# A fused threshold attention and MLP mixer: four PSUM banks shared out anew between values, turned x and the MLPs

## The chip, the cores and the metric

The kernel runs on one core of one Trainium2 chip. The metric is the device time in microseconds (us), the median of three runs. A profiled execution is a separate run, with its own time; the profile's span goes from the first to the last instruction of the program.

## The reference

For each of 8 batch rows there are 8 heads with 576 tokens and 64 features per head. Attention with a threshold comes first, then a mixer's token MLP and channel MLP, all in float32:

```python
scores = scale * np.matmul(q, k.transpose(0, 1, 3, 2))
thresh = np.max(scores, axis=-1, keepdims=True) - tau
scores = np.where(scores >= thresh, scores, -1000000000.0)
scores = scores - np.max(scores, axis=-1, keepdims=True)
attn = np.exp(scores)
attn = attn / (np.sum(attn, axis=-1, keepdims=True) + 1e-09)
x = np.matmul(attn, v)                       # heads side by side: (8, 576, 512)
h = np.maximum(x.transpose(0, 2, 1) @ w_tok1, 0.0) @ w_tok2
u = x + h.transpose(0, 2, 1)
out = u + np.maximum(u @ w_ch1, 0.0) @ w_ch2
```

The token MLP goes 576 to 256 to 576, the channel MLP 512 to 1536 to 512.

## The kernel before, in words

**Units.** Work on attention is cut into 144 units (L85), 18 for each of the 8 rows. A unit is 128 tokens of two heads; of nine units of two pairs of heads the fifth (SHARED, L86) holds the last 64 tokens of both pairs. The loop at L513 goes once through all units and writes out the order of each engine's work by hand (manual_schedule, L81): each engine runs its instructions in the order in which this loop emits them.

**One turn of the loop**, for unit u: `scores(u)` (TensorE's matmuls at L286, VectorE's maximum at L291, GpSimd's bias at L292); `norm(u-1)` (L310 to L314); `turn_blocks(u-2)`, which turns the weights of unit u-2 by VectorE in blocks of 32 (L348) and by 16 DMAs on SyncE's queue (L358), or, for row 0, `turn`, which does it by TensorE through PSUM (L337, L339); `fill(0.4)`; steps of the conversion of the MLPs' weights (`weight`, L544 and L556); `weigh(u)` on ScalarE (Prelu L301 and Exp L304, two each); `fill(0.3)`; `values` for what is due (L549 to L553); `fill(0.3)`; loads.

**Values.** `values(b, p, c)` (L370) multiplies turned weights with v for one pair of heads and 256 tokens, ten matmuls per half (L388, L393), into one tile of pool `ps_tr`; ScalarE copies it into xT (L398). For c == "s", the last 64 tokens, a unit makes two entries in `due` (L541), so `values` is called for pair p and for pair p+1 directly one after the other; these appear as `pv_s` in the profile. All other entries become due in different units.

**MLPs.** When a row's last values have been emitted, `push(b)` (L497) puts that row's MLP steps into `todo`: five of `turn_x` (transposes of x through a `ps_tr` tile, L412, copied by ScalarE, L413), two of `tok1` (L422, Relu on ScalarE L423), eight of `tok2` (L429, added to xT by VectorE, L433), and steps of the channel MLP, `ch1` (L451, Relu on ScalarE L452) and `ch2` (L463 and L467, in four parts that share one tile, copied by VectorE, L472). Steps left over from the row before are interleaved one to one with the new token MLP's (L502 to L504). `fill` takes steps from `todo` by their estimated costs, so that they are spread over the next 17 units; after the last row the rest follows in one stretch. Each tok1, tok2, ch1 and ch2 takes one tile of pool `ps_mm`.

**PSUM.** All matmul results go to PSUM, in tiles of up to 512 floats per partition, one bank each. `ps_sc` (L73) has two tiles of two banks for scores; `ps_tr` (L74) two of one bank; `ps_3rd` (L78) one of two banks, a third scores buffer in row 0 alone. At unit UB = 18, where row 1 begins (L515), `ps_3rd` is closed and `ps_mm` opens with two tiles in its place. A tile of a pool can be written again when the engine that empties it is through with its former use; where a pool's tiles are all in use, the next matmul waits, and so does all that stands behind it on TensorE.

Of the kernel before, what the change touches and what calls it, by code (L numbers as in the profile page):

```python
# [21 lines left out]
def kernel(  # L22
# [48 lines left out]
    work = ctx.enter_context(tc.tile_pool(name="work", bufs=2))  # L71
    small = ctx.enter_context(tc.tile_pool(name="small", bufs=6))
    ps_sc = ctx.enter_context(tc.tile_pool(name="ps_sc", bufs=2, space=bass.MemoryType.PSUM))  # L73
    ps_tr = ctx.enter_context(tc.tile_pool(name="ps_tr", bufs=2, space=bass.MemoryType.PSUM))  # L74


    late = ctx.enter_context(ExitStack())
    ps_3rd = late.enter_context(tc.tile_pool(name="ps_3rd", bufs=1, space=bass.MemoryType.PSUM))  # L78
    ps_mm = None

# [6 lines left out]
    UB = 9 * NP // 2  # L87
# [128 lines left out]
    def weight(n):  # L216

        nonlocal steps_done
        for _ in range(n):
            if next(wops, wops) is wops:  # L220
                return
            steps_done += 1
# [37 lines left out]
    def in_blocks(b):  # L260
        return b > 0
# [10 lines left out]
    def scores(u):  # L272
        b, p0, t = units[u]
        sc = [
            (ps_3rd if b == 0 and (2 * u + h) % 3 == 2 else ps_sc).tile([P, 2, MAIN], F32, tag="sc", name=f"sc{h}_{u}") for h in range(2)
        ]
        if t == SHARED:
            parts = [(b * NP + p0 + i, slice(MAIN, S), slice(64 * i, 64 * i + 64)) for i in range(2)]
        else:
            i, c = divmod(t - (t > SHARED), NI)  # L280
            parts = [(b * NP + p0 + i, slice(P * c, P * c + P), slice(0, P))]
        order = [(f, part, h) for f in range(2) for part in parts for h in range(2)]
        for f, (n, cols, rows), h in order if b else sorted(order, key=lambda o: o[2]):
            r = slice(D * h, D * h + D)
            qT, kT = heads[n]
            nc.tensor.matmul(sc[h][rows, f, 0:HS], lhsT=qT[r, cols], rhs=kT[r, HS * f : HS * f + HS], start=True, stop=True)  # L286
        mx = small.tile([P, 2], F32, tag="mx", name=f"mx_{u}")
        bias = small.tile([P, 2], F32, tag="bias", name=f"bias_{u}")
        for h in range(2):
            c = slice(h, h + 1)  # L290
            nc.vector.tensor_reduce(out=mx[:, c], in_=sc[h][:, :, 0:HS], axis=AX.XY, op=ALU.max)  # L291
            nc.gpsimd.tensor_scalar(out=bias[:, c], in0=mx[:, c], scalar1=toff, scalar2=-SCALE, op0=ALU.add, op1=ALU.mult)  # L292
        st[u] = sc, bias
# [13 lines left out]
    def norm(u):  # L307
        e, rs = st[u]
        rr = small.tile([P, 2], F32, tag="rr", name=f"rr_{u}")
        nc.vector.tensor_scalar(out=rr, in0=rs, scalar1=1e-9, scalar2=None, op0=ALU.add)  # L310
        nc.vector.reciprocal(out=rr, in_=rr)  # L311
        for h in range(2):
            eh = e[:, S * h : S * h + S]
            nc.gpsimd.tensor_scalar(out=eh, in0=eh, scalar1=rr[:, h : h + 1], scalar2=1.0, op0=ALU.mult, op1=ALU.mult)  # L314
        st[u] = e

    def group_of(u):

        b, p0, t = units[u]
        if t == SHARED:  # L320
            return (b, p0, "s"), 0, 1
        i, c = divmod(t - (t > SHARED), NI)
        return (b, p0 + i, c // 2), c % 2, 2

    def turn(u, third):

        key, place, n = group_of(u)
        e = st[u]
        if third == 0 and place == 0:
            eTs[key] = work.tile([P, NK * 2 * P], F32, tag="eT", name=f"eT_{u}")  # L330
        if third == 2:
            st.pop(u)
        eT = eTs[key][:, 0 : NK * n * P].rearrange("p (c x) -> p c x", c=NK)
        ps = ps_tr.tile([P, MAIN], F32, tag="tr", name=f"tr{third}_{u}")[:, 0 : 3 * P].rearrange("p (c x) -> p c x", c=3)
        for c in range(3):
            k0 = (3 * third + c) * P
            nc.tensor.transpose(out=ps[:, c, :], in_=e[:, k0 : k0 + P], identity=ident)  # L337
        on = nc.scalar.copy if third == 1 and u % 2 else nc.vector.tensor_copy
        on(out=eT[:, 3 * third : 3 * third + 3, P * place : P * place + P], in_=ps)  # L339

    def turn_blocks(u):

        key, place, n = group_of(u)
        e = st.pop(u)
        if place == 0:
            Ts[key] = work.tile([P, NK * 2 * P], F32, tag="T", name=f"T_{u}")
        T = Ts[key][:, 0 : NK * n * P]
        nc.vector.transpose(  # L348
            out=T.rearrange("p (a c n x) -> p c a n x", a=4, c=NK, n=n)[:, :, :, place, :],
            in_=e.rearrange("p (c a x) -> p c a x", c=NK, a=4),  # L350
        )
        if place == n - 1:
            del Ts[key]
            eTs[key] = work.tile([P, NK * 2 * P], F32, tag="eT", name=f"eT_{u}")
            w = NK * n * 32
            for a in range(4):
                for i in range(4):
                    nc.sync.dma_start(  # L358
                        out=eTs[key][32 * a : 32 * a + 32, w * i : w * i + w], in_=T[32 * i : 32 * i + 32, w * a : w * a + w]
                    )  # L360

    def split_middle(n):

        lv, vl = vals[n], vlast[n % VL]
        for h in range(2):
            r = slice(D * h, D * h + D)
            nc.gpsimd.tensor_copy(out=vl[r, r], in_=lv[r, NI, :])
        vals[n] = lv, vl
# [118 lines left out]
    def fill(share):  # L487
        nonlocal credit
        credit += share * quota
        while todo and credit > 0:  # L490
            cost, step = todo.popleft()
            credit -= cost
            step()
        if not todo:
            credit = 0.0

    def push(b):  # L497
        nonlocal quota
        uT = xTs[b]
        steps, old = token_mlp(b), list(todo)  # L500
        todo.clear()
        for i in range(max(len(steps), len(old))):  # L502
            todo.extend(old[i : i + 1])
            todo.extend(steps[i : i + 1])  # L504
        for i in range(2) if b % 2 == 0 else range(2, (2 * S + GR - 1) // GR):
            todo.extend(channel_mlp(b - b % 2, uT, i))
        quota = (sum(c for c, _ in todo) - (KEEP if b else 0.0)) / (UB - 1)
# [4 lines left out]
    LAG = 2  # L512
    for u in range(len(units) + LAG + 4):  # L513
        on = u < len(units)
        if u == UB:  # L515
            late.close()
            ps_mm = ctx.enter_context(tc.tile_pool(name="ps_mm", bufs=2, space=bass.MemoryType.PSUM))
        if on:
            b_now, p0, t = units[u]
            n = b_now * NP + p0  # L520
        w = u - LAG
        back = 0 <= w < len(units)
        if on:
            scores(u)
        if 0 < u <= len(units):
            norm(u - 1)
        if back:
            key, place, many = group_of(w)
            if in_blocks(key[0]):
                turn_blocks(w)  # L530
            else:
                for i in range(3):
                    turn(w, i)
            if place == many - 1:
                b, p, c = key
                if c == 0 and p % 2 == 0:
                    split_middle(b * NP + p)
                if c == "s":
                    split_middle(b * NP + p + 1)
                when = u + (2 if in_blocks(b) else 1)  # L540
                due += [(when, b, p + i, c) for i in range(2 if c == "s" else 1)]  # L541
        if b_now:
            fill(0.4)
        weight(4 if b_now else 1)  # L544
        if on:
            weigh(u)
        if b_now:
            fill(0.3)
        while due and due[0][0] <= u:  # L549
            _, b, p, c = due.popleft()  # L550
            values(b, p, c)
            if p == NP - 1 and c == 1:
                push(b)  # L553
        if b_now:
            fill(0.3)
        weight(3 if b_now else 1)  # L556
        if on:
            m = n + 2 + t // 4
            if t < 8 and m < len(pairs):
                load_qk(m, (nc.scalar if b_now else nc.sync,) * 2, t % 4)  # L560
                if t % 4 == 3:
                    load_v(m)
            if t == 2:
                prep(n + 1)
            if t == 7 and n + 2 < len(pairs):
                prep(n + 2)
# [31 lines left out]
```

## Time and profile before

| what | value |
|---|---|
| median of three runs | 1418.58 us (1417.44 to 1421.64) |
| profiled execution, its own time | 1424.03 us |
| its span | 1421.9 us |
| granted TensorE clock, mean | 0.984 |
| VectorE busy | 584.1 us |
| ScalarE busy | 589.8 us |
| GpSimd busy | 345.4 us |
| L398, copies of values: 128x256 | 64, mean 373 ns |
| L291, maximum of scores on VectorE | 288, mean 751 ns |
| L451, ch1 matmuls | 1920, 406.2 us busy |
| L467, ch2 matmuls | 864, 389.5 us busy |

How to read it: PE is TensorE's matmuls, PEld its weight loads, DVE VectorE, ACT ScalarE, POOL GpSimd, SP SyncE, which here only issues DMAs. A row names a line of the kernel, an engine, an operation, what is written and read (out<-in) and the shapes; then come the busy time, the mean duration, and the engine's idle time just before such instructions with what ended most of it. Each float32 matmul of the code shows as two matmul instructions in the profile, a transpose as one. "PE t L429 <- DVE xT L433" means that a matmul at L429 had to wait until an instruction at L433 on VectorE ended. The clock is given as a share of full speed.

### The profile page before, as it was taken

The page shows a single profiled execution, that of the slowest core. Times are in us where ns is not written, and L with a number is a line of the kernel's source. Part 1 is how long each engine was busy: PE and PEld are TensorE (multiplying, and loading weights), DVE is VectorE, ACT ScalarE, POOL GpSimd, SP SyncE. Part 2 cuts the span into 40 slices and gives each one's busy share as a digit, 9 for nine tenths or more (in the row PEclk, how much of TensorE's full clock was granted, in tenths as well). Part 3 has the DMA queues.
Part 4 walks back from the last instruction along what each step waited for, and adds up shares of the span by engine and source line. Part 5 has one row for each costly group of instructions (what it writes and reads, how often), then busy time and mean ns, then how long its engine had stood idle before and what let it go on. Part 6 is the DMA issues. An engine that isn't in the chain of part 4 may idle for free.

```text
span 1421.9 us, 19495 instructions
## 1 busy us (share of the span) xinstructions
PE 1346.7 (95%) x6866; PEld 832.4 (59%) x6866; DVE 584.1 (41%) x1009; ACT 589.8 (41%) x1328; POOL 345.4 (24%) x681
## 2 busy tenths in 40 slices
PE   6777689988999999999999999999999999999998
PEld 4443455645656566565656566566657466566675
DVE  5888654344344443434433444334333443201000
ACT  5776353443545444353434444353334344220110
POOL 4565332222222222222212222222121222100000
PEclk9998899989999999999999999999999999999999
DMA  6344544443444434443343534443433433300000
GB/s 130 90 117 131 152 125 103 92 116 84 102 120 111 108 84 106 104 98 80 92 101 77 121 80 111 104 98 69 103 87 83 111 91 78 82 15 15 8 8 23
DMA packets 257376, 128.34 MB, mean 90 GB/s; under 512 B 208064, under 2 KB 221376, under 8 KB 257280
## 3 DMA queue, kind: packets, MB, share of 16 engines
q1 hardware_dynamic: 131632, 111.46, 29.9%
q10 hardware_dynamic: 125648, 15.64, 6.9%
q8 instruction: 55, 0.90, 0.3%
q14 instruction: 41, 0.34, 0.1%
HBM read 43.25 MB, written 9.44 MB: 37 GB/s over the span
## 4 chain that ended last, share of the span: by engine, by line
PE 81%; DVE 8%; SPq 5%; DMA 3%; ACT 3%; issue 1%; POOL 0%; DVEq 0%; ACTq 0%
PE c L467 26%; PE c L451 24%; PE sc L286 10%; PE pv L393 7%; SPq L358 5%; PE t L422 3%; PE t L429 3%; DVE mx L291 3%; PE pv L388 2%; DVE T L348 2%; PE tx L412 2%; PE c L463 1%; DMA eT<-T 1%; DMA scratch<-in_moe_w_ch_dram 1%; ACT e L301 1%
## 5 line engine op out<-in xcount | busy, mean ns | idle before, releaser
L451 PE MATMUL c<-xT,wc 128*128 128x256 f32 (+1 forms) x1920 | 406.2, 363 | 1.9 <-DVE xT L433 0.8
L291 DVE TENSOR_REDUCE mx<-sc 128x1 f32<-128x576 f32 x288 | 204.6, 751 | 489.5 <-PE sc L286 489.4
L467 PE MATMUL c<-wc,g 128*128 128x512 f32 x864 | 389.5, 597 | 0.0
L451 PEld LDWEIGHTS c<-xT,wc 128*128 128x128 f32 x1920 | 331.7, 190 | 75.9 <-issue 29.9
L292 POOL TENSOR_SCALAR bias<-mx,toff 128x1 f32<-128x1 f32 x288 | 76.7, 267 | 807.8 <-DVE mx L291 754.1
L301 ACT ACTIVATE e<-sc,bias 128x576 f32<-128x576 f32 x288 | 199.2, 741 | 169.7 <-POOL bias L292 148.8
L467 PEld LDWEIGHTS c<-wc,g 128*128 128x128 f32 x864 | 157.6, 190 | 177.3 <-issue 175.9
L452 ACT ACTIVATE g<-c 128x256 f32<-128x256 f32 (+1 forms) x240 | 87.3, 364 | 386.0 <-PE c L451 366.5
L304 ACT ACTIVATE e<-e,ntau 128x576 f32<-128x576 f32 x288 | 220.8, 774 | 0.0
L314 POOL TENSOR_SCALAR e<-e,rr 128x576 f32<-128x576 f32 x288 | 213.4, 753 | 17.3 <-DVE rr L311 4.1
L286 PE MATMUL sc<-kT,qT 64*128 64x288 f32 (+1 forms) x1280 | 196.7, 441 | 20.0 <-ACT e L301 10.9
L348 DVE STREAM_TRANSPOSE T<-e 128x1152 f32<-128x1152 f32 x126 | 172.5, 1369 | 16.5 <-DMA eT<-T 10.8
L286 PEld LDWEIGHTS sc<-kT,qT 64*128 64x128 f32 (+1 forms) x1280 | 107.1, 181 | 102.1 <-issue 50.1
L393 PE MATMUL pv<-eT,lv 128*64 128x256 f32 x1024 | 124.0, 385 | 0.0
L472 DVE COPY o<-c 128x512 f32<-128x512 f32 x36 | 24.6, 684 | 192.7 <-PE c L467 192.7
L393 PEld LDWEIGHTS pv<-eT,lv 128*64 128x64 f32 x1024 | 75.7, 140 | 38.0 <-issue 2.6
L429 PE MATMUL t<-w,a 128*128 128x288 f32 x256 | 78.8, 437 | 17.8 <-DVE xT L433 15.8
L422 PE MATMUL t<-x,w 128*128 128x512 f32 (+1 forms) x160 | 76.0, 613 | 0.0
L429 PEld LDWEIGHTS t<-w,a 128*128 128x128 f32 x256 | 46.7, 197 | 42.6 <-DVE xT L433 20.8
L398 ACT COPY xT<-pv 128x256 f32<-128x256 f32 x64 | 23.9, 373 | 107.4 <-PE pv L393 107.3
L433 DVE TENSOR_TENSOR xT<-xT,t 128x288 f32<-128x288 f32 x64 | 27.9, 442 | 96.5 <-PE t L429 96.4
L304 ACT ACTIVATION_READ_ACCUMULATOR e<-e,ntau 128x1 f32 x288 | 57.4, 199 | 0.0
(43 smaller groups left out, 600.4 us busy)
## 6 DMA issues: line engine op xcount, KB each, us to landing
eT<-T SPq DMA_DIRECT2D x896, 72.0 KB, 2.0
scratch<-in_moe_w_ch_dram SPq DMA_DIRECT2D x24, 512.0 KB, 3.8
lv<-in_v_dram SPq DMA_DIRECT2D x32, 288.0 KB, 3.3
out_dram<-o SPq DMA_DIRECT2D x36, 256.0 KB, 2.2
eT<-T SPq DMA_DIRECT2D x224, 36.0 KB, 1.9
lk<-in_k_dram ACTq DMA_DIRECT2D x108, 72.0 KB, 2.7
lq<-in_q_dram ACTq DMA_DIRECT2D x104, 72.0 KB, 2.1
lq<-in_q_dram SPq DMA_DIRECT2D x24, 72.0 KB, 3.3
```

Of the source, the lines that this page charges most:

```text
L286: nc.tensor.matmul(sc[h][rows, f, 0:HS], lhsT=qT[r, cols], rhs=kT[r, HS * f : HS * f + HS], start=True, stop=True)
L291: nc.vector.tensor_reduce(out=mx[:, c], in_=sc[h][:, :, 0:HS], axis=AX.XY, op=ALU.max)
L301: nc.scalar.activation(out=eh, in_=sc[h][:, :, 0:HS], func=AF.Prelu, bias=bias[:, h : h + 1], scale=SCALE, alpha=STEEP)
L304: nc.scalar.activation(out=eh, in_=eh, func=AF.Exp, bias=ntau, accum_out=rs[:, h : h + 1])
L314: nc.gpsimd.tensor_scalar(out=eh, in0=eh, scalar1=rr[:, h : h + 1], scalar2=1.0, op0=ALU.mult, op1=ALU.mult)
L348: nc.vector.transpose(out=T.rearrange("p (a c n x) -> p c a n x", a=4, c=NK, n=n)[:, :, :, place, :], in_=e.rearrange("p (c a x) -> p c a ...
L393: nc.tensor.matmul(to[r], lhsT=lv[:, j, :], rhs=eT[:, j], start=False, stop=(c == NI - 1), skip_group_check=True)
L422: nc.tensor.matmul(ps, lhsT=w1[0:M, t, P * m : P * m + P], rhs=s["x"][0:M, t, :], start=(t == 0), stop=(t == NT - 1))
L429: nc.tensor.matmul(ps, lhsT=s["a"][:, m, P * c : P * c + P], rhs=w2[:, m, HS * f : HS * f + HS], start=(m == 0), stop=(m == NTK - 1))
L451: nc.tensor.matmul(ps, lhsT=wc1[:, j, c, :], rhs=uT[:, c, GR * i : GR * i + n], start=(c == 0), stop=(c == NCC - 1))
L452: nc.scalar.activation(out=s["g"][:, j, 0:n], in_=ps, func=AF.Relu)
L467: nc.tensor.matmul(flat, lhsT=s["g"][:, j, P * t : P * t + P], rhs=wc2[:, j, :], start=False, stop=(j == NJ - 1), skip_group_check=True)
```

## The change

`ps_tr` is opened in the stack of pools that is closed later, under the name ps_tr0, still with two tiles; it serves row 0. The switch of pools moves from the top of unit 18 to the place just before `push(0)`, in unit 20, after row 0's last values have been emitted. From there on `ps_tr` has one tile and `ps_mm` three. Row 0's values and row 0's turned weights use ps_tr0; row 0's turned x, and values and turned x of all later rows, use the single tile. `ps_sc` stays as it is. No instruction is added, removed or reordered.

```diff
-    ps_tr = ctx.enter_context(tc.tile_pool(name="ps_tr", bufs=2, space=bass.MemoryType.PSUM))
+
 
 
     late = ctx.enter_context(ExitStack())
+    ps_tr = late.enter_context(tc.tile_pool(name="ps_tr0", bufs=2, space=bass.MemoryType.PSUM))
     ps_3rd = late.enter_context(tc.tile_pool(name="ps_3rd", bufs=1, space=bass.MemoryType.PSUM))
     ps_mm = None
...
-        if u == UB:
-            late.close()
-            ps_mm = ctx.enter_context(tc.tile_pool(name="ps_mm", bufs=2, space=bass.MemoryType.PSUM))
...
             values(b, p, c)
             if p == NP - 1 and c == 1:
+                if b == 0:
+                    late.close()
+                    ps_tr = ctx.enter_context(tc.tile_pool(name="ps_tr", bufs=1, space=bass.MemoryType.PSUM))
+                    ps_mm = ctx.enter_context(tc.tile_pool(name="ps_mm", bufs=3, space=bass.MemoryType.PSUM))
                 push(b)
```

## The prediction

> **What bounds the kernel now.** I read the page first, then TensorE's list of waits, then the instructions in order of time at the places where tiles of the two pools that change follow each other. Four lines of the page:
>
> ```profile
> PE 1346.7 (95%) x6866; PEld 832.4 (59%) x6866; DVE 584.1 (41%) x1009; ACT 589.8 (41%) x1328; POOL 345.4 (24%) x681
> ...
> PEclk9998899989999999999999999999999999999999
> ...
> PE 81%; DVE 8%; SPq 5%; DMA 3%; ACT 3%; issue 1%; POOL 0%; DVEq 0%; ACTq 0%
> ...
> L429 PE MATMUL t<-w,a 128*128 128x288 f32 x256 | 78.8, 437 | 17.8 <-DVE xT L433 15.8
> ```
>
> TensorE is busy 95% of the span and 81% of the chain that ended last, at full clock in nearly all of the 40 slices. A change of PSUM pools adds no instruction, so it can only move TensorE's waits. The stage list says where waits are left: 250 to 1300 us has TensorE busy 1033.10 of 1050.00 us, while 107 to 178 us (the beginning of row 1) has it busy only 50.26 of 71. In the long stretch each microsecond that TensorE stands still is a microsecond of the result. All its waits after 200 us:
>
> ```profile
> PE pv L388 <- DMA eT<-T: 5.5, 2, 4.9
> PE t L429 <- DVE xT L433: 4.8, 6, 1.6
> PE sc L286 <- ACT e L301: 3.3, 2, 2.0
> PE t L429 <- ACT g L452: 1.8, 5, 0.4
> PE c L451 <- DVE xT L433: 0.8, 1, 0.8
> ```
>
> (columns: who waited for whom, us in all, times, longest). Waits of t L429 and c L451 for L433 or L452 are waits for a ps_mm bank: tok2 reads nothing that L433 writes. That is 7.4 us, all the idle time that a third ps_mm bank can take away after 200 us. Waits for a ps_tr bank do not appear here at all: two banks are always enough. The question is what one does.
>
> [...] a 0.21 us copy of a finished tile starts only after four activations that were queued earlier. [...] before, the second values group indeed runs before the first is copied. [...] after a wait of 2.0 us it granted 0.50 from 194.60 to 198.00, after one of 1.32 us again from 324.30 to 327.70, and yet after one of 1.60 us (338.59) it did not.
>
> **The change part by part.** (1) *Values and turned x on one bank.* A group on ps_tr may now begin only when ScalarE has copied the group before it. From row 1 on these groups come one at a time, in different units, except in the shared unit: there L550 runs values twice in a row (heads p and p+1 of the last 64 tokens). That is two pairs a row, 14 in rows 1 to 7. TensorE at one of them:
>
> ```profile
> 494.63 0.34 PE L388 MATMUL pv_s<-eT,vl 128*64 128x64 f32 x4
> 494.80 0.64 PE L393 MATMUL pv_s<-eT,lv 128*64 128x64 f32 x16
> 495.26 0.29 PE L388 MATMUL pv_s<-eT,vl 128*64 128x64 f32 x4
> 495.38 0.64 PE L393 MATMUL pv_s<-eT,lv 128*64 128x64 f32 x16
> ```
>
> and ScalarE at the same time:
>
> ```profile
> 494.74 0.60 ACT L423 ACTIVATE a<-t 128x512 f32<-128x512 f32 x1 [6.56 <-PE t L422]
> 495.23 1.37 ACT L301 ACTIVATE e<-sc,bias 128x576 f32<-128x576 f32 x2
> 496.48 0.79 ACT L304 ACTIVATE e<-e,ntau 128x576 f32<-128x576 f32 x1
> ...
> 497.24 0.78 ACT L304 ACTIVATE e<-e,ntau 128x576 f32<-128x576 f32 x1
> ...
> 498.00 0.33 ACT L398 COPY xT<-pv_s 128x64 f32<-128x64 f32 x2
> ```
>
> (start us, us, instruction). The second group starts at 495.26. With one bank it waits for the first copy, 498.00 + 0.21 = 498.21: 2.95 us, plus the 0.05 us that lie between the end of a copy and the matmul that it releases (copy over at 126.46, matmul at 126.51). Behind it on TensorE stands everything else, the next scores too, and nothing covers it. I measured all 14 pairs like this. Where ScalarE is free (281.39, 574.44, 653.79, 740.56, 980.80, 1066.85, 1226.10) the wait is 0.43 us: 7 x 0.43 = 3.0. Where the copy is behind the unit's Exp (203.25, 357.34, 896.69: 1.29 each; 423.13: 1.10) it is 5.0. Where tok1's Relu holds back all of weigh (495.26, 821.30, 1147.63) it is 2.95 each, 8.9. With 14 x 0.05 = 0.7 the **pairs cost 17.5 us**.
>
> Turned x: at the end of row 1 (312.52) five tx groups follow pv(row end) at 0.9 us distance or less, since the copy of one lies under the transposes of the next. On one bank each takes its transposes (0.6 to 0.9), the copy (0.59) and two hand-overs: I get 313.04 for the first and 317.6 in place of 315.6 for the end of the fourth, **2.0 us**. In later rows push interleaves them with older steps, and five collisions are left: 470.69 and 795.25 (0.53 each), 614.72 and 938.27 (the copy waits behind weigh, 1.72 each), 1119.66 (0.74): **5.2 us**. In row 0's chain tx 0 now waits for the copy as well (it ran at 121.17, ahead of the 4.7 us wait), and tx 1 to 4 follow 1.3 to 1.5 us apart and not 0.9: 2.7 us. TensorE waits 8.0 us for VectorE soon after, so part may vanish there: between 0 and 2.7, I take **1.5**.
>
> (2) *Three banks for the MLPs.* After 350 us the bank waits sum to 4.8 us; [...] nearly all of them are waits for the group just before, so a free bank removes them: **-6**. The two 1.60 us waits of row 2 (338.59, 346.68) are a third tok2 waiting for the first's add, which VectorE reaches late. A third bank lets one more tok2 of 0.97 us run; then the fourth waits: **-1.9**. Row 1's waits of 8.0 and 3.0 us are the same, but VectorE there is held at 151.14 by a weight load, so again one tok2 moves into the wait. It ran at half clock afterwards (eight matmuls from 152.72 took 4.21 us, 2.1 per tok2), so 2.1 + 1.9 at most; I take **-3**, between 0 and 18 (both waits and the half clock after them gone). The sum is -11, from -6 to -26.
>
> (3) *The clock.* Nine waits of over 1 us appear in stretches at full clock. Each may cost a 3.4 us window at half clock, 1.7 us. Of the waits of 1.3 to 2.0 us that the trace has after 180 us about half were followed by such a window. I count three quarters for the three long ones and 0.3 for six shorter: 4 windows, **+7**, from 0 to 15.
>
> (4) *The switch moved from unit 18 to 20* costs nothing: ps_mm is first used after push(0) either way, and turned x of row 0 needs the last values of that row anyhow. Evictions stay where they are in the queues; no DMA moves.
>
> Sum: 17.5 + 2.0 + 5.2 + 1.5 - 11 + 7 = +22 us on the profiled execution of 1424.03 us (span 1421.9). That execution lies 5.45 us above the median, so 1424.03 + 22 - 5.45 = **1440.6 us**, which I give as 1440. Its own range, with the pairs and the row 1 and later tx waits (24.7) as measured: from +7 (row 0's chain 0, gains 18, clock 0) to +34 (2.7, 6 and 13), 1426 to 1453.
>
> **The rivals.** *The clock becomes the bound* (slower still): every one of the nine waits draws a half-clock window, 9 x 1.7 = 15.3, and gains stay at 6: 17.5 + 7.2 + 2.7 - 6 + 15.3 = +37, 1455. For it speaks the window at 324.30 after only 1.32 us idle; against it the three waits of 1.6 to 1.75 us without one.
>
> *Row 1 gives back more than the pairs take* (faster). Row 1 is the one stage where TensorE is idle by tens of microseconds, because tok2 stands before the next scores in its queue. If one more bank lets these scores go early enough, 8.0 + 3.0 us and the half clock after them (10.24 and 3.41 us at 0.50, so 6.8) go, with 8 of the rest: -26. If row 1 and 2 also swallow their own pairs (4.1 with 203.25, 281.39, 357.34 and 423.13) and tx chains (3.5), 17 us of cost is left before the clock's: -9, 1410. It decides if over two thirds of the 11 us go. Against it: the add is released by a weight load, not by a bank.
>
> *A draw*: gains of about 19 (bank waits of the page, 15.8 + 1.8 + 0.8 + 0.6) against 24.7 without any clock loss, part absorbed: +2, 1420.
>
> That the pools do not do what they say can be excluded for ps_tr: with bufs=1 no second bank exists.
>
> **How the numbers follow.** Forecast 0.62, clock 0.20, draw 0.10, row 1 faster 0.08. The range 1424 to 1455 takes in the forecast, the clock case and the upper part of the draw. A measurement of this kernel can tell about 0.3% (4.3 us) from no change: faster 0.08, same 0.10, slower 0.82.
>
> **What would show it.** Right: in TensorE's waits a new row, pv_s L388 for ACT xT L398, 14 times and 15 to 18 us, longest near 3; tx L412 for ACT x L413; t L429 for DVE xT L433 down to a few us after 200 us; some more half-clock windows. Wrong: no such row, or 107 to 178 us much shorter, or pairs far from 1.2 us in the mean because the order of ScalarE's work has shifted.

## The result and the profile after

The changed kernel takes 1445.08 us (median of 5 runs, 1442.14 to 1447.06); before took 1420.28 us beside it (5 runs, 1417.44 to 1421.64). The ratio is 1.0166, 95% interval 1.014 to 1.0192: 24.8 us slower. The forecast was 1440 us, on a median of 1418.58.

From the pages: in the changed kernel's file every line from the pool definitions on has moved down by one, so tok2 is L430 and not L429, and its add L434.

```profile
PE 1351.5 (94%) x6866; PEld 837.2 (58%) x6866; DVE 583.1 (40%) x1009; ACT 589.3 (41%) x1328; POOL 346.8 (24%) x681
...
L430 PE MATMUL t<-w,a 128*128 128x288 f32 x256 | 75.0, 421 | 7.9 <-DVE xT L434 7.9
```

No engine has other work: the counts are equal, and busy times differ by under 5 us. The span grew from 1421.9 to 1443.0 us. tok2's idle time before its matmuls fell from 17.8 to 7.9 us: the third bank did what it was there for. What was added is in TensorE's waits after 200 us (who waited for whom, us in all, times, longest):

```profile
PE pv_s L389 <- issue: 14.8, 13, 2.9
PE tx L413 <- ACT x L414: 5.1, 5, 1.6
PE pv L389 <- DMA eT<-T: 4.4, 1, 4.4
PE sc L287 <- ACT e L302: 3.3, 2, 2.0
PE tx L413 <- ACT xT L399: 1.4, 3, 0.5
PE pv_s L389 <- POOL wc L169: 1.2, 1, 1.2
PE pv L389 <- issue: 0.7, 1, 0.7
PE c L452 <- DVE xT L434: 0.6, 1, 0.6
PE t L430 <- DVE xT L434: 0.6, 1, 0.6
```

The first row is new and is the largest: 13 waits before the second values group of a pair, and the 14th is the row with L169, 16.0 us in all. The list does not name the releaser here ("issue", and once a GpSimd instruction that has nothing to do with it); the instructions in order of time do. TensorE at the pair that the prediction showed:

```profile
507.10 0.34 PE L389 MATMUL pv_s<-eT,vl 128*64 128x64 f32 x4 [2.87 <-issue]
507.23 0.67 PE L394 MATMUL pv_s<-eT,lv 128*64 128x64 f32 x16
507.83 2.08 PE L452 MATMUL c<-xT,wc 128*128 128x128 f32 x8
```

and ScalarE:

```profile
506.03 0.78 ACT L305 ACTIVATE e<-e,ntau 128x576 f32<-128x576 f32 x1
506.69 0.20 ACT L305 ACTIVATION_READ_ACCUMULATOR e<-e,ntau 128x1 f32 x1
506.79 0.21 ACT L399 COPY xT<-pv_s 128x64 f32<-128x64 f32 x1
507.94 0.21 ACT L399 COPY xT<-pv_s 128x64 f32<-128x64 f32 x1 [0.94 <-PE pv_s L394]
```

The first copy ends at 507.00 behind the second Exp, and the second group starts at 507.10. Before, both copies ran back to back behind the Exp (0.33 us from 498.00), and TensorE had begun on the ch1 matmuls behind them at 495.95. Behind the wait the granted clock is 0.50 from 507.80 to 511.20 us, and eight ch1 matmuls take 2.08 us where they took 1.16.

Where the 21.1 us of span come from can be read by taking the two traces (one execution each) matmul by matmul, since the order on TensorE is the same in both. The table has the differences of start-to-start times, in us; the 14 pairs come to more than their 16.0 us of waits because each place loses another 0.16 us beside the wait:

| place | measured | in the prediction |
|---|---|---|
| 14 pairs: 7 x 0.53, 3 x 1.38, 1.23, 3.04 + 3.05 + 3.04 | +18.2 | 17.5 |
| turned x in row 1's end (0.73, 0.70, 0.63) | +2.1 | 2.0 |
| five later turned x collisions (0.54, 1.72, 0.54, 1.72, 0.79) | +5.3 | 5.2 |
| turned x of row 0 | +3.8 | 1.5, from 0 to 2.7 |
| tok2 in row 1 (-8.20, -0.40 and +5.98; -3.18 and +1.15) | -4.7 | -3 |
| tok2 in row 2 (-1.76 + 0.79, -1.77 + 0.80) | -1.9 | -1.9 |
| MLP bank waits after 350 us, those over 0.3 us | -5.9 | -6 |
| granted clock of 0.50, four stretches from 330 us on (1.6, 1.6, 0.87, 0.90) | +5.0 | 7 |

These sum to +21.9. Another 2.0 us of the span lie before row 1, where the two programs are the same, so they are scatter between two executions, and the rest (-2.8) is in smaller pieces, some of opposite sign, which I did not attribute. The prediction's -6 for the MLP banks stands on 4.8 us of waits; the rest of it was an estimate of such a loss beside each wait.

### The profile page after: what moved, and what is told of

The parts are those of the page before. It is cut to its first block, busy times and chain, and to the rows that moved or that the text cites. A ratio compares the mean times of both kernels' runs of the same rounds, so it can differ in the third digit from the quotient of the medians.

```text
span 1443.0 us, 19520 instructions
## 1 busy us (share of the span) xinstructions
PE 1351.5 (94%) x6866; PEld 837.2 (58%) x6866; DVE 583.1 (40%) x1009; ACT 589.3 (41%) x1328; POOL 346.8 (24%) x681
## 4 chain that ended last, share of the span: by engine, by line
PE 85%; DVE 5%; DMA 2%; ACT 2%; SPq 2%; issue 2%; POOL 1%; ACTq 0%; DVEq 0%; POOLq 0%
PE c L468 26%; PE c L452 26%; PE sc L287 10%; PE pv L394 7%; PE t L423 5%; PE t L430 4%; PE pv L389 2%; SPq L359 2%; PE tx L413 2%; DVE mx L292 2%; PE c L464 1%; PE pv_s L394 1%; DMA scratch<-in_moe_w_ch_dram 1%; DVE scratch L165 1%; ACT e L302 1%
## 5 line engine op out<-in xcount | busy, mean ns | idle before, releaser
L287 PE MATMUL sc<-kT,qT 64*128 64x288 f32 (+1 forms) x1280 | 199.8, 446 | 21.8 <-ACT e L302 12.5
L430 PE MATMUL t<-w,a 128*128 128x288 f32 x256 | 75.0, 421 | 7.9 <-DVE xT L434 7.9
L430 PEld LDWEIGHTS t<-w,a 128*128 128x128 f32 x256 | 45.8, 192 | 29.2 <-issue 10.1
L434 DVE TENSOR_TENSOR xT<-xT,t 128x288 f32<-128x288 f32 x64 | 27.1, 440 | 87.8 <-PE t L430 87.8
```

The costliest lines, as they stand in the source:

```text
L430: nc.tensor.matmul(ps, lhsT=s["a"][:, m, P * c : P * c + P], rhs=w2[:, m, HS * f : HS * f + HS], start=(m == 0), stop=(m == NTK - 1))
```

## The experiments

Each was timed beside the kernel before on the same chip, and its ratio is to that; the brackets give the 95% interval. Each is made from the changed kernel. A difference between two of these ratios is known to some 0.003, or 4 to 5 us.

**late_switch**: the switch in unit 20, the old numbers of tiles.

```diff
-ps_tr = ...tile_pool(name="ps_tr", bufs=1, ...)
-ps_mm = ...tile_pool(name="ps_mm", bufs=3, ...)
+ps_tr = ...tile_pool(name="ps_tr", bufs=2, ...)
+ps_mm = ...tile_pool(name="ps_mm", bufs=2, ...)
```

> The pools change in unit 20 as in the changed kernel, but with two tiles each, as before. Theory (only the bank counts matter): the time of before, 1420 us, within 0.3%, no wait of pv_s. Rival (the later switch itself costs, because the new pools must wait for row 0's last tiles): 3 us or more above before, with new waits of TensorE between 115 and 135 us.

Measured 1422.81 us against 1423.28, ratio 1.0000 (0.9989 to 1.0011). Between 115 and 135 us its two waits are those that before has there (turned x for the copy, 5.3 us and 4.7 before; scores, 3.4 us in both). The moved switch costs nothing that can be measured; what the changed kernel loses comes with the numbers of tiles.

**one_and_two**: one ps_tr tile, and ps_mm back to two.

```diff
-ps_mm = ...tile_pool(name="ps_mm", bufs=3, ...)
+ps_mm = ...tile_pool(name="ps_mm", bufs=2, ...)
```

> One ps_tr tile, two ps_mm tiles, one bank unused: the loss without the gain. Theory: the changed kernel's time plus what the third ps_mm bank returned (9 to 11 us): about 1455 us, pv_s waits of 18 us as in the changed kernel, t L430 waits for L434 back to some 16 us. Rival (the third bank returned nothing, its waits only moved): 1445 us, the same as the changed kernel.

Measured 1457.3 us, ratio 1.0246 (1.0228 to 1.0265). Against the changed kernel's 1.0166 that is 0.0080, about 11 us: what the third ps_mm bank returns. Its waits over the whole span show the pairs as they were and tok2's back:

```profile
PE pv_s L389 <- issue: 16.0, 14, 2.9
...
PE t L430 <- DVE xT L434: 14.4, 6, 7.1
...
PE t L430 <- ACT g L453: 1.8, 5, 0.4
```

So the loss alone is about 35 us (0.0246 of 1420) and the gain alone about 11.

**pairs_apart**: the second group of a shared unit becomes due one unit later.

```diff
-due += [(when, b, p + i, c) for i in range(2 if c == "s" else 1)]
+due += [(when + i, b, p + i, c) for i in range(2 if c == "s" else 1)]
```

> The changed kernel, with the second values group of each shared unit made one unit later, so that the first one's copy is long done. Theory: the 14 pair waits go (18.2 us by comparing the two traces) and with them the half-clock windows after the three waits of 3 us (3 x 1.7 us): about 1422 us. Rival (ScalarE's queue or other work is the bound and the wait reappears elsewhere): over 1435 us.

Measured 1427.88 us, ratio 1.0040 (1.0026 to 1.0054): 0.0126, or 18 us, less than the changed kernel, where 23 were expected. Its waits after 200 us have no row of pv_s any more, and its granted clock is 0.978 in the mean, where the changed kernel has 0.973. The time returned is thus the pairs' in kind, but 5 us less than expected, about as much as the noise. The traces give three reasons for it: the three stretches at 0.50 behind the long waits had cost 3.4 us and not 5.1 (table above), two new waits of the scores for ScalarE appear (4.5 us in 4 waits, where the changed kernel has 3.3 in 2), and a group that stood alone took more of TensorE's time than one directly behind another (0.93 us and 0.58, merged_tx_in_mm below).

**tx_in_mm**: turned x in a ps_mm tile.

```diff
-ps = ps_tr.tile([P, MAIN], F32, tag="tr", name=f"tx_{b}_{t}")...
+ps = ps_mm.tile([P, MAIN], F32, tag="mm", name=f"tx_{b}_{t}")...
```

> The changed kernel, with turned x in a ps_mm tile in place of ps_tr. Theory: the collisions of turned x go (about 11 us gross in the trace, the part in row 0's chain partly covered), pairs stay: 1436 to 1440 us. Rival (turned x then takes the banks that the MLPs gained): 1445 us or more, with t L430 or c L452 waits back.

Measured 1435.58 us, ratio 1.0085 (1.0065 to 1.0104), 0.0081 or 11.5 us less than the changed kernel, a little better than expected. Waits after 200 us:

```profile
PE pv_s L389 <- issue: 14.8, 13, 2.9
...
PE c L452 <- ACT x L414: 2.2, 2, 1.1
```

The pair row is to the digit that of the changed kernel; of the turned x waits, ch1 takes over 2.2 us, in two waits of 1.1, where it now meets the bank of a turned x that ScalarE has not copied. Row 0's chain of turned x gave 3.6 us back at once (four times 0.88 to 0.94). TensorE's next long wait for VectorE grew by 0.8 us only (6.1 to 6.9), so the cover that the prediction saw for the chain in that wait was small.

**apart_tx_in_mm**: both edits.

> Pairs a unit apart and turned x in a ps_mm tile, both on the changed kernel. Theory (the two losses are separate and add up): the changed kernel less 19 (pairs_apart) less 11 (tx_in_mm): 5 to 6 us under before, ratio 0.996. Rival (the two savings overlap, or the second values group and turned x now wait for each other's data): ratio 1.000 or more.

Measured 1418.94 us, ratio 0.9983 (0.9973 to 0.9994). Had the savings added up exactly, it would be 0.9959 (1.0166 less 0.0126 and 0.0081). Some 3 us are missing, which the noise of these four ratios does not tell from nothing; that the two savings are separate fits, and is not shown to the microsecond.

**merged_tx_in_mm**: turned x in ps_mm, and the two groups side by side in one tile, copied once.

```diff
+pair = c == "s" and b > 0
+if pair and p % 2 == 0:
+    pair_ps[0] = ps_tr.tile([P, MAIN], F32, tag="tr", ...)
+whole = pair_ps[0] if pair else ps_tr.tile(...)
+ps = whole[:, first : first + N] if pair else whole[:, 0:N]
...
-nc.scalar.copy(out=x, in_=ps)
+if not pair:
+    nc.scalar.copy(out=x, in_=ps)
+elif p % 2:
+    x = xTs[b][:, p - 1 : p + 1, ...]
+    nc.scalar.copy(out=x, in_=whole[:, 0 : 2 * N].rearrange("p (a x) -> p a x", a=2))
```

> Turned x in ps_mm tiles, and the two values groups of a shared unit beside each other in one ps_tr tile, copied once for both. Theory: no pair wait, and 14 copies fewer on ScalarE, which is not the bound: like apart_tx_in_mm within 2 us, ratio 0.995 to 0.997. Rival (the order of the pairs mattered in apart_tx_in_mm): differs from it by more than 4 us.

Measured 1410.89 us, ratio 0.9929 (0.9910 to 0.9948): 8 us faster than apart_tx_in_mm, so the rival of this run held. From the first scores of row 2 to TensorE's last matmul this kernel's trace has 1120.4 us and that of apart_tx_in_mm 1130.4. Taken matmul by matmul, these 10 us have four parts. 3.3 us lie from 321.0 to 327.8 us, where that execution had the lower clock (granted from 200 to 1290 us: 0.99 there, 1.00 here). 1.5 us are three waits that are longer there, two of them of the scores for ScalarE (0.6 each). 0.6 us come from where the count begins, in the middle of a pair. The remaining 4.6 us are 13 times 0.35 us, with no idle time of TensorE: a second group directly behind the first held up the matmuls after it by 0.58 us, and the same group alone, one unit later, by 0.93. So pulling the pairs apart had a price of its own here, 4.9 us for 14 of them as an estimate from this figure. What in TensorE makes it was not tested. This run also has 14 copies fewer on ScalarE, and what that alone is worth was not tested either.

**pair_copy_dve**: the pairs' copies on VectorE.

```diff
-nc.scalar.copy(out=x, in_=ps)
+(nc.vector.tensor_copy if key[2] == "s" else nc.scalar.copy)(out=x, in_=ps)
```

> The changed kernel, with the copies of the last 64 tokens' values on VectorE in place of ScalarE, row 0's too. Theory (a pair's wait is one copy plus what ScalarE has queued before it): 14 waits stay, each about 0.5 us as where ScalarE was free, 7 to 8 us in all in place of 18.2, and the half-clock windows after the long ones go: 12 to 14 us under the changed kernel, ratio to before 1.007 to 1.009. Rival (the wait is a price of the bank's hand-over itself): no change, ratio 1.016.

Measured 1432.4 us, ratio 1.0086 (1.0064 to 1.0109), 11.4 us less than the changed kernel. The first two rows of its waits after 200 us:

```profile
PE tx L413 <- ACT x L414: 5.1, 5, 1.6
PE pv_s L389 <- issue: 4.9, 13, 0.4
```

The waits are all still there, 13 in one row and one under another name, and none is longer than 0.4 us, about what they had where ScalarE was free. Here the bank set how often TensorE waited (14 times in both kernels), the queue in front of the copy how long (up to 2.9 us there, up to 0.4 here).

**one_pool**: values, turned x and MLPs from one pool of four.

```diff
-ps_tr = ctx.enter_context(tc.tile_pool(name="ps_tr", bufs=1, ...))
-ps_mm = ctx.enter_context(tc.tile_pool(name="ps_mm", bufs=3, ...))
+ps_tr = ps_mm = ctx.enter_context(tc.tile_pool(name="ps_mm", bufs=4, ...))
...
-tag="tr" (values, turned x)
+tag="mm" (row 0's values keep "tr")
```

> From row 1 on values, turned x and all MLP tiles take any of four banks of one pool; order of instructions unchanged. Theory (what costs is a bank that is not there when it is needed, not the number of banks in all): no pair wait, no turned x wait, nearly no wait of the MLPs: 8 to 12 us under before, ratio 0.992 to 0.994. Rival (MLP tiles that wait for their copies hold all four banks when values come): ratio over 0.999, with new pv waits.

Measured 1404.58 us, ratio 0.9887 (0.9867 to 0.9907): faster than both kernels, and than expected. All waits of TensorE after 200 us:

```profile
PE pv L389 <- DMA eT<-T: 4.8, 2, 4.0
PE sc L287 <- ACT e L302: 3.3, 2, 2.0
PE pv_s L389 <- ACT e L305: 0.3, 1, 0.3
```

But for 0.3 us, whose releaser the list does not settle, no wait for a bank of this pool is left; of the other two rows 7.3 us lie between 280 and 340 us, around the end of row 1. Why the gain is larger than the 8 to 12 us expected was not taken apart.

**one_pool_of_3**: the same with three tiles.

> As one_pool, with three tiles and one bank unused: as many banks as in one_and_two (one and two), but open to all. Theory (the loss comes from how the banks are tied to tiles, not from their number): most of one_pool's time is kept, ratio to before 0.992 to 1.000, pair waits well under 5 us. Rival (three banks are too few, the fourth one is what one_pool gains by): ratio 1.010 or more, near one_and_two's 1.0246.

Measured 1413.72 us, ratio 0.9937 (0.9919 to 0.9955): three banks open to all beat four banks tied two and two (before), and beat three banks tied one and two (one_and_two) by 0.031. They are as fast as merged_tx_in_mm (0.9929), which has four banks tied one and three but takes away the pairs' waits by other means.

## Why the prediction was right

**The pairs** (17.5 against 18.2): right in number, place and each length. Each wait is 0.05 us longer than forecast, since the hand-over from copy to matmul was put at 0.05 us and is 0.10 here (507.00 to 507.10). That the long ones are made by the queue in front of the copy is shown by pair_copy_dve: all 14 shrink to 0.4 us.

**Turned x** (8.7 against 11.2): right in the later rows (5.2 against 5.3, 2.0 against 2.1). The term mis-sized is row 0's chain, bounded by 2.7 and taken at 1.5; it cost 3.8. Two things failed. First, the groups followed each other 1.8 us apart and not 1.3 to 1.5 (130.17, 131.96, 133.75, at a granted clock of 0.50; in row 1's end, at 1.00, they were 1.33 apart). Second, the prediction counted on TensorE's wait for VectorE to cover part of it; VectorE is held there by a weight load (idle for 4.28 us before, 3.14 in the changed kernel), and this cover would need the load to come at a fixed time. It came later too: VectorE went on at 151.14 us before and at 157.36 in the changed kernel. SyncE issues the load right behind the 16 DMAs of turned weights, and these started 6.5 us later. Before:

```profile
136.82 10.06 SPq L358 DMA_DIRECT2D eT<-T  x16
146.98 1.02 SPq L196 DMA_DIRECT2D scratch<-in_moe_w_ch_dram  x2
```

In the changed kernel:

```profile
143.34 10.07 SPq L359 DMA_DIRECT2D eT<-T  x16
153.52 1.02 SPq L197 DMA_DIRECT2D scratch<-in_moe_w_ch_dram  x2
```

Behind this stands the chain itself. The DMAs follow work of VectorE, and VectorE waits for a step that ScalarE has queued behind its copies of turned x: the last of these ended at 130.69 before and at 137.22 in the changed kernel, and VectorE stood idle until 131.85 and until 138.37. So a delay of the chain is carried on to the load and hardly covered. tx_in_mm agrees: without the waits of the chain TensorE comes to that wait 6.5 us earlier than in the changed kernel and leaves it 5.6 us earlier (153.29 against 158.93).

**The third bank** (-11 against -12.5; one_and_two gives about 11): right, and so was the expectation that row 1's waits would shrink and not vanish. The 8.0 us before the third tok2 became 6.1 before the fourth. one_pool shows what a fourth open bank does there: all four tok2 run at once, and TensorE then waits 6.3 us for ScalarE at the next scores; VectorE stands idle for a weight load until 151.30 (4.05 us), as ScalarE did in before until 151.13 (7.11 us). So the rival in which row 1 gives back over two thirds of its 11 us did not come true: row 1's tok2 gave 4.7. (That rival's sum is also off: 26.2 less 4.1 and 3.5 leaves 18.6 us of cost and not 17, which changes nothing.)

**The clock** (7 against 5.0): each of the three long waits (2.9 us) was followed by 3.4 us at a granted clock of 0.50, from 507.8, 838.9 and 1170.0, and none of the six shorter ones (1.21 to 1.55 us) was. Yet a wait of 1.32 us that is in both traces was followed by a clock of 0.50 in both, from 324.30 before and from 330.3 in the changed kernel, so these traces show no length of wait that decides it, and the prediction's shares of three quarters and 0.3 were an estimate. The three cost 1.6, 0.87 and 0.90 us and not 1.7 each. In the two cheaper ones the scores held 2.2 us of TensorE's time where before, at a granted clock of 1.00, they had held 1.8; in the first one it was 1.8 in place of 1.2. The rival in which every wait of over 1 us is followed by such a stretch falls too.

**The switch**: nothing, as late_switch shows.

The sum was +22 on the profiled execution (1424.03), which gives 1446; the changed kernel's profiled execution took 1445.19. That they agree to 1 us is in part luck: the pairs and turned x were together 3.2 us too small, the third bank 1.5 too small and the clock 2.0 too large, and the measured difference also holds 2.0 us of scatter and -2.8 that was not attributed. The range of 1426 to 1453 took gains of 18 and a clock loss of 13, where the terms themselves allowed 26 and 15. The deduction of 5.45 us for the median rested on three runs; five runs of before have a median 1.7 us higher, which is part of why the forecast lies 5 us under the result.

## What to carry to other kernels

Before taking a buffer from a pool, list every place where two of its tiles follow each other on the bound engine, and read for each when the emptying engine gets to the first: the sum of these waits is the price, and here it depended on that engine's queue more than on the copy (a copy of 0.21 us made waits of 0.4 to 2.9). Here buffers of one size that serve streams with different rhythms were worth more in one pool than divided: with the order of work unchanged, both splits of four that were tried (two and two, one and three) lost to three in common (ratios of 1 and 1.0166 against 0.9937). Where two small results always come together, try one tile and one copy for both: here no wait of these groups was left after 200 us, without a second buffer (merged_tx_in_mm). And before counting on a wait elsewhere to cover a delay, see whether what ends it starts later too: here the weight load came 6.2 us later.

## What the runs showed that I had not expected

Moving a 64-token group away from its neighbour on TensorE cost 0.35 us each time with no wait involved (merged_tx_in_mm). A stretch of 3.4 us at a granted clock of 0.50 cost as little as 0.87 us. And a weight load by DMA, which looks like an event of its own time, came 6.2 us later because copies on ScalarE were late, through VectorE and SyncE's queue.
